# Late pairs of heads: split numerators, GpSimd low parts, queries ranked one pair earlier, one set of inputs

## The chip, the cores and the metric

The kernel runs on one core of one Trainium2 chip. Its engines are TensorE (PE in the profile, with its weight loads shown apart as PEld), VectorE (DVE), ScalarE (ACT), GpSimd (POOL) and SyncE (SP), which here only starts DMAs. The metric is the device time of one execution in microseconds; lower is better.

## The reference

First a linear attention with exponential features over 8 batches, 8 heads, 576 tokens and head size 64, then a gated feed-forward layer over the 4608 tokens that come out (width 512, hidden width 1536). All of it is float32.

```python
def phi(x):
    proj = np.einsum('bhsd,df->bhsf', x, w_phi)              # 64 -> 128 features
    proj = proj - np.max(np.abs(proj), axis=-1, keepdims=True)
    return np.concatenate([np.exp(proj), np.exp(-proj)], axis=-1)
q_p, k_p = phi(q), phi(k)
kv  = einsum('bhsf,bhsd->bhfd', k_p, v);  z = k_p summed over s
num = einsum('bhsf,bhfd->bhsd', q_p, kv)
den = einsum('bhsf,bhf->bhs', q_p, z)[..., None] + 1e-06
x   = num / den                                              # 4608 x 512
g   = x @ w_gate
out = (silu(g) * (x @ w_val)) @ w_out
```

## The kernel before

**Parts.** TensorE multiplies either float32, which it records as two instructions for each product, or `float32r`, one instruction. For a product in `float32r` that keeps the accuracy, both factors are written as a high part (a rounding copy) and a low part (value minus high part), and three products are added: high by high, low by high, high by low. The feed-forward layer has been done so throughout; the attention in parts of it.

**Attention.** Two heads make a pair, and there are 32 pairs, four for each batch. `attention(i, rank)` (from line 370) writes out pair i. The key side: load keys and values, project the keys in three groups into PSUM, find the largest magnitude (L447), subtract it (L452), two exponentials (L456, L457), products with the values into one PSUM bank `ps_kv` (L465, L472), then copy the sums out to `kvs` (L493, called `kvc`). The query side of a late pair: for each head a high part by ScalarE (L551) and a low part by VectorE (L553) into `qs`, two projections, copies to `qx` by ScalarE (L566), transpose, reduce, six tiny operations over groups of partitions (L582 to L587), transpose back (L591), subtract (L594), two exponentials (L596, L598) into `qe` and `qx`. Then the numerators and denominators: for each head two parts of 288 tokens, each of them two float32 products of `kvs` with `qe` and `qx`; ScalarE copies them out (L620, L622); VectorE divides (L629 to L633). The result is stored to DRAM or split into `xh` and `xl` (L655, L657).

**Early and late.** Pairs 0 to 7 are early and use float32 and another query path. Pairs 8 to 31 are late: keys (from pair 9) and queries are split into parts, the numerators are float32. Late pairs use two sets of inputs `kin`, `qin`, `vf` in turn, two sets of `qx`, `qe` and of `kvs`, and one set of `ks`, `qs`.

**Order.** All steps are given to a planner (`Plan`) with the engine, an assumed cost, what they wait for, and a rank. It runs through an assumed time line, and each engine always takes the ready step of lowest rank; the resulting order is what each engine then executes, strictly in that order. A late pair's steps have the pair's number as rank; steps that free a PSUM bank have a rank near -0.8 (`freeing`), feed-forward steps off TensorE -1 or -0.5. Feed-forward products on TensorE have ranks above 1000, so that they fill what the attention leaves free. Late pairs have two PSUM banks (`work`) for projections and numerators together; a step with `take` holds one until the step with `give`.

**Stages.** Early pairs come first, then the weights are decoded from float64, while feed-forward products of the first chunks of 384 tokens fill TensorE; then the late pairs with products of chunks 0 to 5; then chunks 6 to 11, two at a time, with seven products in place of eight (`pair`, L1006), for which GpSimd makes combined weights (L913, L918) and VectorE and ScalarE combined inputs (L951 to L955). These may only begin after the last step of the attention (`ended`). SBUF of the stages is shared in areas `m1`, `m2`, `a1`, `a2` by `view(tag, shape, dtype, when)`.

Of the kernel before, what the change touches and what calls it, by code (L numbers as in the profile page):

```python
# [17 lines left out]
P = 128  # L18
S = 576
# [29 lines left out]
ROOM = {"m1": 6912, "m2": 5140, "a1": 2432, "a2": 2048}  # L49
URGENT = -0.8  # L50
T_SETS = 2
# [144 lines left out]
def favor_attention_moe(ctx: ExitStack, tc: tile.TileContext, qT, kT, v, w_phi, wg, wv, wo, out):  # L196
# [58 lines left out]
    kvs = [view("m2", [4 * P]) for _ in range(2)]  # L255
    qy = [view("m2", [4, NF]) for _ in range(2)]
# [11 lines left out]
    shared = [view("a1", [2 * DM], U32) for _ in range(2)] + [view("a2", [2 * DM]) for _ in range(2)]  # L268
    raw = [t.rearrange("p (n t) -> p n t", t=2) for t in shared[:2]]
    we, wa = ([t[:, i * DM:(i + 1) * DM] for i in range(2)] for t in shared[2:])  # L270
    ks, qs = view("a1", [2, SK], F32R, 1), view("a1", [2, S], F32R, 1)
    for t, shape in ((kin, [SK]), (qin, [SK]), (vf, [5, 2, D2])):
        t[1] = view("a2", shape, F32, 1)
# [97 lines left out]
    def attention(i, rank):  # L371
# [4 lines left out]
        one = 0 if early else j  # L376
# [4 lines left out]
        if i == EARLY_PAIRS + 1:  # L381
            def clear():
                nc.gpsimd.memset(vf[1]()[:, :, :, D:], 1.0)
                for h in range(2):
                    nc.gpsimd.memset(vf[1]()[h * D:(h + 1) * D, 4, 1 - h], 0.0)
                    nc.gpsimd.memset(kin[1]()[h * D:(h + 1) * D, 4 * P + (1 - h) * D:4 * P + (2 - h) * D], 0.0)

            last["vf", i - 2] = last["kin", i - 2] = last["qin", i - 2] = add("POOL", 1000, clear, weights_done, rank)
        before = lambda name: [last.get((name, i - (1 if i <= EARLY_PAIRS else 2)))]

        k_in = [add("SP", P * 4 * P * 4, lambda: nc.sync.dma_start(get(kin[one])[:, :4 * P], kT[b, pr, :, :4 * P]),
                    before("kin"), rank)]
        k_in += [add("SP", P * P, lambda r=slice(h * D, (h + 1) * D), c=4 * P + h * D: nc.sync.dma_start(
            get(kin[one])[r, c:c + D], kT[b, pr, r, 4 * P:]), before("kin"), rank) for h in range(2)]
        if early:
            q_in = [add("SP", P * 4 * P * 4, lambda: nc.sync.dma_start(get(qin[one])[:, :4 * P], qT[b, pr, :, :4 * P]),
                        before("qin"), rank)]
            q_in += [add("SP", P * P, lambda r=slice(h * D, (h + 1) * D), c=4 * P + h * D: nc.sync.dma_start(
                get(qin[one])[r, c:c + D], qT[b, pr, r, 4 * P:]), before("qin"), rank) for h in range(2)]
        else:  # L400
            q_in = [add("SP", P * S * 4, lambda: nc.sync.dma_start(get(qin[one])[:, :S], qT[b, pr]), before("qin"), rank)]
# [10 lines left out]
        if plain:  # L412
            k_ready = k_in
        else:
            k_hi = add("ACT", act(SK), lambda: nc.scalar.copy(ks()[:, 0], get(kin[one])),
                       [*k_in, last.get(("khi", i - 1)), *weights_done], rank)
            k_lo = add("DVE", dve(SK), lambda: vec.tensor_tensor(
                out=ks()[:, 1], in0=get(kin[one]), in1=ks()[:, 0], op=ALU.subtract), [k_hi], rank)
            k_ready = [k_hi, k_lo]
            last["kin", i] = k_lo  # L420
        kv_steps = []
        for g, (t0, t1) in enumerate(GROUPS):
# [9 lines left out]
            def project(t0=t0, t1=t1, key=key, tail=tail):  # L432
                o = work[plan.bank[key]]
                for t in range(t0, t1):
                    c = slice(t * P, (t + 1) * P)
                    acc = o[:, :NF] if tail else o[:, (t - t0) * 256:(t - t0 + 1) * 256]
                    if plain:
                        matmuls([(acc, get(kin[one])[:, c], wst if tail else wbd, True, True)])
# [6 lines left out]
            kproj = add("PE", w * (pe32(width) if plain else 3 * pe(width)), project, k_ready, rank, take=key)  # L445
# [5 lines left out]
            def centre(n=n, m=m, view=view, room=room):  # L451
# [4 lines left out]
            e0 = add("ACT", act(n * NF), lambda x=room: nc.scalar.activation(x[:, :, 0], x[:, :, 1], AF.Exp), [ksub], rank)  # L456
            e1 = add("ACT", act(n * NF), lambda x=room: nc.scalar.activation(x[:, :, 1], x[:, :, 1], AF.Exp, scale=-1.0),  # L457
                     [e0], rank)
            last["km", 3 * i + g] = ksub

            def values(t0=t0, t1=t1, room=room, tail=tail):
                kv_open[0] = not tail
                if tail:
                    for k in range(2):
                        nc.tensor.matmul(ps_kv[:, 2 * k * D2:2 * (k + 1) * D2], room[:, 0, k],  # L465
                                         get(vf[one])[:, 4].rearrange("p h d -> p (h d)"), start=False, stop=k == 1)
                    return
                for t in range(t0, t1):
                    for h in range(2):
                        for k in range(2):  # L470
                            o = ps_kv[:, (2 * k + h) * D2:(2 * k + h + 1) * D2]
                            nc.tensor.matmul(o, room[:, 2 * (t - t0) + h, k], get(vf[one])[:, t, h], start=t + h + k == 0, stop=False)  # L472

            kv = add("PE", 2 * n * pe32(D2), values, [e1, *v_in, last.get(("kv", i - 1)), *kv_steps[-1:]], rank)
# [24 lines left out]
        if early:  # L499
            for g, (t0, t1) in enumerate(GROUPS):  # L500
# [9 lines left out]
                def project(t0=t0, t1=t1, key=key, tail=tail):  # L510
                    o = work[plan.bank[key]]
                    for t in range(t0, t1):
                        x = get(qin[one])[:, t * P:(t + 1) * P]
# [33 lines left out]
        else:  # L547
            copies, q_lo = [], []
            for h in range(2):
                ra, rb = rows(h)  # L550
                hi = add("ACT", act(S), lambda h=h, ra=ra: nc.scalar.copy(qs()[ra, h], get(qin[one])[ra, :S]),  # L551
                         [*q_in, last.get(("qs", h, i - 1)), *weights_done], rank)
                lo = add("DVE", dve(S), lambda h=h, ra=ra, rb=rb: vec.tensor_tensor(  # L553
                    out=qs()[rb, h], in0=get(qin[one])[ra, :S], in1=qs()[ra, h], op=ALU.subtract), [hi], rank)
# [320 lines left out]
    for t in (hh, hl):  # L875
        t += [view(tag, [CH], F32R, 2) for tag in ("a1", "m1")]
# [269 lines left out]
```

## Time and profile before

| | |
|---|---|
| Time, median of 3 runs | 1262.28 us (1261.77 to 1264.46) |
| The profiled execution's own time | 1262.5 us |
| Its span from first to last instruction | 1260.7 us |
| Mean granted TensorE clock | 0.997 |
| Busy share: PE, DVE, ACT, POOL | 98%, 75%, 55%, 20% |
| Late pairs on TensorE | from about 285 us to 797 us |
| First product of chunks 6 to 11 | 826.97 us |

A group's row gives line, engine, operation, output and input tiles by name, shape and count, then busy time, mean time of one, and idle time ahead of it with what ended it. Tiles that are views of a shared area appear under the first letter of the area's name: `m` for `m1` and `m2`, `a` for `a1` and `a2`. L312 is the helper that issues most matmuls. A row of a stretch gives start and end, its length, and for each engine the busy time and the instructions. A matmul's recorded time includes its way through the array, so the spacing of starts is what one costs TensorE.

### The profile page before, as it was taken

The page shows a single profiled execution, that of the slowest core. Times are in us where ns is not written, and L with a number is a line of the kernel's source. Part 1 is how long each engine was busy: PE and PEld are TensorE (multiplying, and loading weights), DVE is VectorE, ACT ScalarE, POOL GpSimd, SP SyncE. Part 2 cuts the span into 40 slices and gives each one's busy share as a digit, 9 for nine tenths or more (in the row PEclk, how much of TensorE's full clock was granted, in tenths as well). Part 3 has the DMA queues.
Part 4 walks back from the last instruction along what each step waited for, and adds up shares of the span by engine and source line. Part 5 has one row for each costly group of instructions (what it writes and reads, how often), then busy time and mean ns, then how long its engine had stood idle before and what let it go on. Part 6 is the DMA issues. An engine that isn't in the chain of part 4 may idle for free.

```text
span 1260.7 us, 19274 instructions
## 1 busy us (share of the span) xinstructions
PE 1241.0 (98%) x7008; PEld 1145.7 (91%) x7008; DVE 943.2 (75%) x1674; ACT 688.3 (55%) x1419; POOL 246.9 (20%) x306
## 2 busy tenths in 40 slices
PE   9999999999999999999999999989999999999998
PEld 8898899999888999999999999979998999989997
DVE  7997799997878888777877967586557756575553
ACT  6887333337677767666766765443334433353333
POOL 0000000000000000000000000285565665565550
PEclk9999999999999999999999999999999999999999
DMA  4433455546463424443444332632213322222211
GB/s 147 134 115 91 144 183 175 172 161 204 147 193 109 139 92 129 117 132 122 121 123 128 126 108 71 211 133 76 74 52 113 117 72 76 76 101 75 76 51 51
DMA packets 107312, 149.26 MB, mean 118 GB/s; under 512 B 52048, under 2 KB 61776, under 8 KB 107216
## 3 DMA queue, kind: packets, MB, share of 16 engines
q1 hardware_dynamic: 106752, 147.76, 37.3%
q8 instruction: 55, 0.90, 0.3%
q14 instruction: 41, 0.34, 0.1%
q10 hardware_dynamic: 464, 0.26, 0.1%
HBM read 119.67 MB, written 28.31 MB: 117 GB/s over the span
## 4 chain that ended last, share of the span: by engine, by line
PE 90%; DVE 4%; POOL 2%; DMA 1%; ACT 1%; issue 1%; SPq 0%; DVEq 0%; POOLq 0%
PE gv L312 23%; PE gv L1006 19%; PE o L312 19%; PE work L312 17%; PE kv L472 8%; PE kv L312 2%; PE kv L465 1%; POOL a L913 1%; POOL a L918 1%; DMA a<-in_wg_dram 1%; DVE m L951 0%; PE o L534 0%; DVE xl L955 0%; DMA m<-wlo_dram 0%; DVE km L447 0%
## 5 line engine op out<-in xcount | busy, mean ns | idle before, releaser
L312 PE MATMUL gv<-xh,w_hi 128*128 128x384 f32 x576 | 201.6, 350 | 1.4 <-DVE th L742 1.4
L312 PE MATMUL gv<-xl,w_hi 128*128 128x384 f32 x576 | 193.2, 335 | 0.0
L312 PE MATMUL gv<-xh,w_lo 128*128 128x384 f32 x576 | 193.2, 335 | 0.0
L1006 PE MATMUL gv<-xh,m 128*128 128x384 f32 x504 | 151.3, 338 | 2.6 <-ACT m L1014 2.5
L913 POOL TENSOR_TENSOR a<-w_hi,m 128x256 f32<-128x256 f32 x48 | 40.0, 865 | 571.9 <-DMA m<-wlo_dram 564.1
L918 POOL TENSOR_TENSOR a<-a 128x256 f32<-128x256 f32 x144 | 117.5, 816 | 8.5
L312 PEld LDWEIGHTS gv<-xh,w_hi 128*128 128x128 f32 x576 | 108.3, 188 | 5.1 <-DVE th L742 2.0
L312 PE MATMUL o<-w_hi,hh 128*128 128x512 f32 x270 | 112.1, 415 | 0.0
L913 POOL TENSOR_TENSOR a<-w_hi,w_lo 128x256 f32<-128x256 f32 x96 | 88.8, 954 | 118.2 <-DMA w_lo<-wlo_dram 96.1
L312 PEld LDWEIGHTS gv<-xl,w_hi 128*128 128x128 f32 x576 | 108.3, 188 | 3.2 <-DVE xl L657 0.2
L1017 DVE TENSOR_TENSOR a<-gv,a 128x384 f32<-128x384 f32 x72 | 39.9, 553 | 94.4 <-PE gv L1006 94.2
L312 PE MATMUL work<-m,m 128*128 128x288 f32 x408 | 109.4, 406 | 0.0
L312 PEld LDWEIGHTS gv<-xh,w_lo 128*128 128x128 f32 x576 | 108.1, 188 | 0.0
L312 PE MATMUL o<-w_hi,hl 128*128 128x512 f32 x270 | 107.1, 397 | 0.0
L1006 PEld LDWEIGHTS gv<-xh,m 128*128 128x128 f32 x504 | 93.7, 189 | 5.7 <-ACT m L1014 3.3
L312 PE MATMUL o<-w_lo,hh 128*128 128x512 f32 x243 | 95.7, 394 | 0.0
L312 PEld LDWEIGHTS work<-m,m 128*128 128x128 f32 x408 | 76.5, 189 | 17.1
L1006 PE MATMUL gv<-xh,w_hi 128*128 128x384 f32 x216 | 73.7, 341 | 7.5 <-DVE a L1017 4.9
L765 ACT CAST hh<-th 128x384 fp32r<-128x384 f32 x108 | 55.3, 512 | 44.0 <-DVE th L745 30.6
L472 PEld LDWEIGHTS kv<-m,m 128*128 128x128 f32 x640 | 75.8, 192 | 2.5 <-ACT m L457 0.8
L472 PE MATMUL kv<-m,m 128*128 128x66 f32 x640 | 75.6, 273 | 0.8 <-ACT m L457 0.6
L1006 PE MATMUL gv<-xl,w_hi 128*128 128x384 f32 x216 | 73.4, 340 | 0.0
(183 smaller groups left out, 2958.9 us busy)
## 6 DMA issues: line engine op xcount, KB each, us to landing
w_lo<-wlo_dram SPq DMA_DIRECT2D x60, 512.0 KB, 3.6
w_lo<-wlo_dram SPq DMA_DIRECT2D x78, 256.0 KB, 3.1
wlo_dram<-w_lo SPq DMA_DIRECT2D x36, 256.0 KB, 2.1
out_dram<-osb SPq DMA_DIRECT2D x30, 256.0 KB, 2.7
a<-in_wg_dram SPq DMA_DIRECT2D x12, 512.0 KB, 3.7
a<-in_wv_dram SPq DMA_DIRECT2D x12, 512.0 KB, 3.6
a<-in_wo_dram SPq DMA_DIRECT2D x12, 512.0 KB, 3.6
m<-wlo_dram SPq DMA_DIRECT2D x12, 512.0 KB, 3.6
```

Source lines behind the costliest of these rows:

```text
L312: nc.tensor.matmul(o, l, r, start=a, stop=z)
L465: nc.tensor.matmul(ps_kv[:, 2 * k * D2:2 * (k + 1) * D2], room[:, 0, k], get(vf[one])[:, 4].rearrange("p h d -> p (h d)"), start=False, st ...
L472: nc.tensor.matmul(o, room[:, 2 * (t - t0) + h, k], get(vf[one])[:, t, h], start=t + h + k == 0, stop=False)
L765: s4 = add("ACT", act(CH), lambda: nc.scalar.copy(get(hh[b]), th[j]), [made, hid_free[b]], FIRST)
L913: gp.tensor_tensor(out=full()[:, block(n)], in0=hi[:, block(n)], in1=get(low)[:, block(n)], op=ALU.add)
L918: gp.tensor_tensor(out=x[:, block(o)], in0=x[:, block(l)], in1=x[:, block(r)], op=ALU.subtract)
L1006: nc.tensor.matmul(o[:, :CH], l, r, start=begin and i == 0, stop=i == len(terms) - 1, skip_group_check=True)
L1017: return add("DVE", dve(CH), lambda: vec.tensor_tensor(out=snap[n](), in0=bank_c[:, :CH], in1=snap[n](), op=ALU.add), after, FIRST)
```

## The change

It concerns late pairs, apart from where views lie.

- **Numerators.** `kvs` becomes a high part `kvh` (ScalarE, from PSUM) and a low part `kvl` (VectorE, PSUM minus `kvh`), one set instead of two, made at `freeing` rank. For each head, `qe` and `qx` are copied to high parts `qh` (ScalarE) and their low parts `ql` are made by GpSimd; there is one set of these for both heads. Each part of 288 tokens then takes six `float32r` products instead of two float32 ones. `qx` is free after the low parts instead of after the numerators.
- **GpSimd.** The low parts of keys and queries move from VectorE to GpSimd.
- **Query copies** out of PSUM move from ScalarE to VectorE.
- **Ranks.** Steps of a late pair get one of five offsets; that of the query projections (`rq`) is -1, the others 0.
- **Waits.** A key projection takes its bank only once the feature buffer that it will fill is free, and a query projection only once `qx` is.
- **One set of inputs.** `kin`, `qin`, `vf` are no longer doubled for late pairs; each load waits for the pair before. The GpSimd memsets for the second set go.
- **Areas.** `a2` goes, `b1` comes; the views of the last stage are spread otherwise.

```diff
-ROOM = {"m1": 6912, "m2": 5140, "a1": 2432, "a2": 2048}
+ROOM = {"m1": 6912, "m2": 3096, "a1": 4096, "b1": 2048}
+OFFSETS = (0, -1, 0, 0, 0)
...
+    qh, ql = ([view("a1", [S], F32R, 1) for _ in range(2)] for _ in range(2))
+    kvh, kvl = view("a1", [4 * P], F32R, 1), view("b1", [4 * P], F32R, 1)
...
+        rk, rq, rm, rn, rt = (rank + (0 if early else o) for o in OFFSETS)
...
-        before = lambda name: [last.get((name, i - (1 if i <= EARLY_PAIRS else 2)))]
+        before = lambda name: [last.get((name, i - 1))]
...
-            k_lo = add("DVE", dve(SK), lambda: vec.tensor_tensor(
-                out=ks()[:, 1], in0=get(kin[one]), in1=ks()[:, 0], op=ALU.subtract), [k_hi], rank)
+            k_lo = add("POOL", pool2(SK), lambda: nc.gpsimd.tensor_tensor(
+                out=ks()[:, 1], in0=kin[0], in1=ks()[:, 0], op=ALU.subtract), [k_hi], rk)
...
-            kproj = add("PE", w * (pe32(width) if plain else 3 * pe(width)), project, k_ready, rank, take=key)
+            kproj = add("PE", w * (pe32(width) if plain else 3 * pe(width)), project,
+                        [*k_ready, *([] if early else [last.get(("kp", 3 * i + g - 2))])], rk, take=key)
...
             kvc.append(add("ACT", act(4 * D), lambda ones=ones: nc.scalar.copy(
-                cut(kvs[j], ones), sums(ones)), [kv_steps[-1], *use("kvs")], rank))
+                cut(kvs[j] if early else kvh(), ones), sums(ones)),
+                [kv_steps[-1], *(use("kvs") if early else [last.get(("kvs", i - 1)), *weights_done])], freeing))
+        if not early:
+            for ones in range(2):
+                kvc.append(add("DVE", dve(4 * D), lambda ones=ones: vec.tensor_tensor(
+                    out=cut(kvl(), ones), in0=sums(ones), in1=cut(kvh(), ones), op=ALU.subtract),
+                    [kvc[ones], last.get(("kvs", i - 1))], freeing))
...
-                lo = add("DVE", dve(S), lambda h=h, ra=ra, rb=rb: vec.tensor_tensor(
-                    out=qs()[rb, h], in0=get(qin[one])[ra, :S], in1=qs()[ra, h], op=ALU.subtract), [hi], rank)
+                lo = add("POOL", pool2(S), lambda h=h, ra=ra, rb=rb: nc.gpsimd.tensor_tensor(
+                    out=qs()[rb, h], in0=qin[0][ra, :S], in1=qs()[ra, h], op=ALU.subtract), [hi], rq)
...
-                    pj = add("PE", 2 * pe(SH), project, [lo], rank, take=key)
-                    copies.append(add("ACT", act(SH), lambda h=h, c=c, key=key: nc.scalar.copy(
+                    pj = add("PE", 2 * pe(SH), project, [lo, *use("qx")], rq, take=key)
+                    copies.append(add("DVE", dve(SH), lambda h=h, c=c, key=key: vec.tensor_copy(
                         qx[j][:, h, c], work[plan.bank[key]][:, :SH]), [pj, *use("qx")], freeing, give=key))
...
+                            terms += [(kvh()[:, n], qh[k]()[:, c]), (kvl()[:, n], qh[k]()[:, c]), (kvh()[:, n], ql[k]()[:, c])]
...
-                nu = add("PE", 2 * pe32(SH), numerators, [*done[h], *kvc, nu], rank, take=key)
+                if not early and part == 0:
+                    for k in range(2):
+                        g0 = add("ACT", act(S), lambda k=k, h=h: nc.scalar.copy(qh[k](), (qe, qx)[k][j][:, h]),
+                                 [(f0, f1)[k][h], nu or last.get(("nu", i - 1)), *weights_done], rn)
+                        done[h] += [g0, add("POOL", pool2(S), lambda k=k, h=h: nc.gpsimd.tensor_tensor(
+                            out=ql[k](), in0=(qe, qx)[k][j][:, h], in1=qh[k](), op=ALU.subtract), [g0], rn)]
+                nu = add("PE", 2 * pe32(SH) if early else 6 * pe(SH), numerators, [*done[h], *kvc, nu], rn, take=key)
...
-        last["qx", i], last["qx'", i] = nu, None
+        last["qx", i], last["qx'", i] = (nu, None) if early else (done[0][-1], done[1][-1])
...
-    t_low, t_high = ([view("m1", [8 * P], F32R, 2) for _ in range(T_SETS)] for _ in range(2))
+    t_low, t_high = ([view("a1", [8 * P], F32R, 2) for _ in range(T_SETS)] for _ in range(2))
...
-    temps = [view("m2", [2, CH], F32, 2) for _ in range(6)]
+    temps = [view("m1", [2, CH], F32, 2) for _ in range(6)]
...
-    lo_bufs = [view("m1", [8 * P], F32R, 2) for _ in range(LOW_SETS - LO_SETS)] + [flat(t) for t in w1_lo]
+    lo_bufs = [view("b1", [8 * P], F32R, 2) for _ in range(LOW_SETS - LO_SETS)] + [flat(t) for t in w1_lo]
```

More of the change, by code (lines that the diff above doesn't have):

```diff
@@ L254, in favor_attention_moe @@
     kp = [view("m1", [2, 2, 2, NF]) for _ in range(2)]
-    kvs = [view("m2", [4 * P]) for _ in range(2)]
-    qy = [view("m2", [4, NF]) for _ in range(2)]
+    kvs = [view("b1", [4 * P]) for _ in range(2)]
+    qy = [view("b1", [4, NF]) for _ in range(2)]
     kin, qin = [view("m2", [SK])] * 2, [view("m2", [SK])] * 2
@@ L265, in favor_attention_moe @@
     osb = sb("osb", [P, DM], F32, 2)
[L268 removed]
+    shared = [view("a1", [2 * DM], U32) for _ in range(2)] + [view("a1", [2 * DM]) for _ in range(2)]
     raw = [t.rearrange("p (n t) -> p n t", t=2) for t in shared[:2]]
     we, wa = ([t[:, i * DM:(i + 1) * DM] for i in range(2)] for t in shared[2:])
[L271 to L273 removed]
+    ks, qs = view("a1", [2, SK], F32R, 1), view("b1", [2, S], F32R, 1)
+    qh, ql = ([view("a1", [S], F32R, 1) for _ in range(2)] for _ in range(2))
+    kvh, kvl = view("a1", [4 * P], F32R, 1), view("b1", [4 * P], F32R, 1)
     def bank(name):
@@ L414, in attention @@
         else:
-            k_hi = add("ACT", act(SK), lambda: nc.scalar.copy(ks()[:, 0], get(kin[one])),
-                       [*k_in, last.get(("khi", i - 1)), *weights_done], rank)
-            k_lo = add("DVE", dve(SK), lambda: vec.tensor_tensor(
-                out=ks()[:, 1], in0=get(kin[one]), in1=ks()[:, 0], op=ALU.subtract), [k_hi], rank)
+            k_hi = add("ACT", act(SK), lambda: nc.scalar.copy(ks()[:, 0], kin[0]),
+                       [*k_in, last.get(("khi", i - 1)), *weights_done], rk)
+            k_lo = add("POOL", pool2(SK), lambda: nc.gpsimd.tensor_tensor(
+                out=ks()[:, 1], in0=kin[0], in1=ks()[:, 0], op=ALU.subtract), [k_hi], rk)
             k_ready = [k_hi, k_lo]
@@ L437, in project @@
                     if plain:
-                        matmuls([(acc, get(kin[one])[:, c], wst if tail else wbd, True, True)])
+                        matmuls([(acc, kin[0][:, c], wst if tail else wbd, True, True)])
                     else:
@@ L471, in values @@
                             o = ps_kv[:, (2 * k + h) * D2:(2 * k + h + 1) * D2]
-                            nc.tensor.matmul(o, room[:, 2 * (t - t0) + h, k], get(vf[one])[:, t, h], start=t + h + k == 0, stop=False)
-            kv = add("PE", 2 * n * pe32(D2), values, [e1, *v_in, last.get(("kv", i - 1)), *kv_steps[-1:]], rank)
+                            nc.tensor.matmul(o, room[:, 2 * (t - t0) + h, k], vf[0][:, t, h], start=t + h + k == 0, stop=False)
+            kv = add("PE", 2 * n * pe32(D2), values, [e1, *v_in, last.get(("kv", i - 1)), *kv_steps[-1:]], rk)
             last["kp", 3 * i + g] = kv
@@ L512, in project @@
                     for t in range(t0, t1):
-                        x = get(qin[one])[:, t * P:(t + 1) * P]
+                        x = qin[0][:, t * P:(t + 1) * P]
                         matmuls([(o[:, :NF], x, wst, True, True) if tail else
@@ L550, in attention @@
                 ra, rb = rows(h)
-                hi = add("ACT", act(S), lambda h=h, ra=ra: nc.scalar.copy(qs()[ra, h], get(qin[one])[ra, :S]),
-                         [*q_in, last.get(("qs", h, i - 1)), *weights_done], rank)
-                lo = add("DVE", dve(S), lambda h=h, ra=ra, rb=rb: vec.tensor_tensor(
-                    out=qs()[rb, h], in0=get(qin[one])[ra, :S], in1=qs()[ra, h], op=ALU.subtract), [hi], rank)
+                hi = add("ACT", act(S), lambda h=h, ra=ra: nc.scalar.copy(qs()[ra, h], qin[0][ra, :S]),
+                         [*q_in, last.get(("qs", h, i - 1)), *weights_done], rq)
+                lo = add("POOL", pool2(S), lambda h=h, ra=ra, rb=rb: nc.gpsimd.tensor_tensor(
+                    out=qs()[rb, h], in0=qin[0][ra, :S], in1=qs()[ra, h], op=ALU.subtract), [hi], rq)
                 q_lo.append(lo)
@@ L571, in attention @@
             turns = [add("DVE", dve(S), lambda h=h: vec.transpose(qe[j][:, h], qx[j][:, h]),
-                         [*copies[2 * h:2 * h + 2], *use("qe")], rank) for h in range(2)]
+                         [*copies[2 * h:2 * h + 2], *use("qe")], rm) for h in range(2)]
             per_head = lambda f: [(lambda h=h: f(h)) for h in range(2)]
```

74 lines of the change are left out of this document (34 added, 40 removed).

## The prediction

> **What bounds the kernel now.** I read the page's chain of waits first, shares of the span by engine, then busy time by stretch (PE, PEld, DVE, ACT, POOL).
>
> ```profile
> PE 90%; DVE 4%; POOL 2%; DMA 1%; ACT 1%; issue 1%; SPq 0%; DVEq 0%; POOLq 0%
> ```
>
> ```profile
> 285.00:797.00 512.00, 512.00 (x3074) 468.89 (x3073) 405.88 (x776) 349.60 (x757) 0.00 (x0) 1.00 0.42 128
> 797.00:827.00 30.00, 27.47 (x144) 25.14 (x142) 20.62 (x26) 10.14 (x17) 14.38 (x13) 0.99 0.63 216
> ```
>
> TensorE sets the end: the chain is 90% PE. In the stretch of the late pairs, the first row, PE is busy for all of 512 us, at the full granted clock (1.00). That is 512 / 24 = 21.3 us a pair, in which VectorE works 405.88 / 24 = 16.9 us (79%), ScalarE 14.6 us, GpSimd nothing. The waits in that stretch say the same from the other side:
>
> ```profile
> PEld work L312 <- DVE m L452: 0.4, 2, 0.2
> ```
>
> ```profile
> DVE m L629 <- ACT m L622: 35.6, 14, 4.7
> ```
>
> TensorE's weight loads waited 0.4 us in all, while VectorE waited 35.6 us for the copies of the numerators alone. The attention is ready when TensorE reaches it, so work taken from TensorE here shortens the run, as long as that stays so.
>
> **The products: what they cost and will cost.** The time line of PE around two heads' numerators, and query projections already made of parts:
>
> ```profile
> 603.72 2.10 PE L312 MATMUL work<-m,m 128*128 128x288 f32 x8
> 605.44 0.61 PE L312 MATMUL o<-w_hi,hh 128*128 128x512 f32 x1
> 605.89 0.39 PE L312 MATMUL o<-w_lo,hh 128*128 128x512 f32 x1
> 606.12 0.40 PE L312 MATMUL o<-w_hi,hl 128*128 128x512 f32 x1
> 606.35 2.10 PE L312 MATMUL work<-m,m 128*128 128x288 f32 x8
> 608.08 0.55 PE L312 MATMUL gv<-xh,w_hi 128*128 128x384 f32 x1
> 608.47 0.34 PE L312 MATMUL gv<-xl,w_hi 128*128 128x384 f32 x1
> 608.64 0.34 PE L312 MATMUL gv<-xh,w_lo 128*128 128x384 f32 x1
> 608.82 0.30 PE L312 MATMUL work<-a,wst_hi 128*128 128x288 f32 x1
> ...
> 609.09 0.34 PE L312 MATMUL gv<-xh,w_hi 128*128 128x384 f32 x1
> ...
> 609.61 0.29 PE L312 MATMUL work<-a,wst_hi 128*128 128x288 f32 x1
> ...
> 609.87 0.34 PE L312 MATMUL gv<-xh,w_hi 128*128 128x384 f32 x1
> ```
>
> A head's numerators now take 605.44 - 603.72 = 1.72 us and 608.08 - 606.35 = 1.73 us. The product right behind them is late too: it holds TensorE for 0.45 us (605.44 to 605.89) where its neighbour takes 0.23, and 0.39 us (608.08 to 608.47) where the next takes 0.17. So a head costs 1.725 + 0.22 = 1.945 us, and 48 heads 93.4 us. After, a head takes 12 products of 288 columns. Those of the query projections, each with a new stationary operand as here, take two in 0.27 us (608.82 to 609.09) and two in 0.26 (609.61 to 609.87), 0.1325 us each; 48 x 12 x 0.1325 = 76.3 us. No switch between kinds is left behind them. **TensorE saves 93.4 - 76.3 = 17.1 us**, 0.7 us a pair. The count of the other products is the same.
>
> **VectorE and ScalarE.** Rows from the groups by form:
>
> ```profile
> L452 DVE TENSOR_TENSOR m<-work,km 128x512 f32<-128x512 f32 x55 | 38.0, 691 | 2.2
> L566 ACT COPY m<-work 128x288 f32<-128x288 f32 x96 | 36.5, 402 | 17.9 <-PE work L312 16.9
> L596 ACT ACTIVATE m<-m 128x576 f32<-128x576 f32 x48 | 31.7, 682 | 11.3 <-DVE m L594 11.2
> L553 DVE TENSOR_TENSOR a<-a,a 64x576 fp32r<-64x576 f32 x24 | 18.1, 753 | 0.7
> L553 DVE TENSOR_TENSOR a<-m,a 64x576 fp32r<-64x576 f32 x24 | 18.1, 753 | 2.5 <-ACT a L551 1.7
> L417 DVE TENSOR_TENSOR a<-a,a 128x640 fp32r<-128x640 f32 x12 | 9.8, 818 | 0.4 <-ACT a L415 0.4
> L417 DVE TENSOR_TENSOR a<-m,a 128x640 fp32r<-128x640 f32 x11 | 9.0, 819 | 0.1
> L452 DVE TENSOR_TENSOR m<-work,km 128x128 f32<-128x128 f32 x31 | 8.6, 276 | 0.2
> ```
>
> VectorE loses the low parts, 18.1 + 18.1 + 9.8 + 9.0 = 55.0 us. It gains 96 query copies of 288 columns out of PSUM; between the two L452 rows a column costs (691 - 276) / 384 = 1.08 ns, so a copy is 276 + 160 x 1.08 = 449 ns and all are 43.1 us; and 48 subtractions of 256 columns at 276 + 128 x 1.08 = 414 ns, 19.9 us. Sum: +8 us, 0.3 us a pair. ScalarE loses the 36.5 us of L566 and gains 96 high parts of 576 at 682 ns, 65.5 us: +29 us, or 1.2 us a pair on 14.6. Neither is on the path while TensorE finds its operands ready; uncovered, they would add 1.5 us a pair, 36 us.
>
> **GpSimd.** It has no work in this stretch now; its only large operation is in the last stage:
>
> ```profile
> L918 POOL TENSOR_TENSOR a<-a x144: 727/739/1457, 811.4 to 1226.2; 128x256 f32<-128x256 f32 x144
> ```
>
> Undisturbed it takes 727 ns for 256 columns. For 576 that gives 1.64 us if all of it grows with the columns, and 0.65 us more than 727 ns, 1.38 us, if it grows at twice VectorE's 1.08 ns; I take 1.55, near the upper end, and 1.7 for 640. Each late pair puts six of the first and one of the second on GpSimd: 11 us a pair, 262 us in all, in a 21 us period. It keeps up. But a head's numerators now follow two copies and two low parts in series (0.68 + 2 x 1.55 = 3.8 us), twice per pair, since the second head reuses `qh` and `ql`: 7.6 us more of latency. The other pair in flight covers it (16.9 us of VectorE work per pair); uncovered it costs 182 us.
>
> **What GpSimd takes from VectorE.** VectorE's lines in the last stage (least, median and longest ns):
>
> ```profile
> L1025 DVE SCALAR_TENSOR_TENSOR th<-th,m x36: 550/1086/1097, 833.5 to 1243.9; 128x384 f32<-128x384 f32 x36
> L1025 DVE SCALAR_TENSOR_TENSOR th<-th,gv x36: 539/554/555, 838.7 to 1249.5; 128x384 f32<-128x384 f32 x36
> L955 DVE TENSOR_TENSOR xl<-m,xh x18: 948/1484/1497, 811.8 to 1117.2; 128x768 fp32r<-128x768 f32 x18
> ```
>
> With both inputs in SBUF and GpSimd at work, 384 columns take 1086 ns in place of 550, and 768 columns 1484 in place of 948. The loss is 536 ns for either length, so it is a wait for one GpSimd instruction, not a lower rate. With one input in PSUM (`gv`) there is none. The Trainium skill, "SBUF — State Buffer", section "Who interferes with whom", has this as a rule: a VectorE instruction with two SBUF inputs and a GpSimd one that reads SBUF take one shared port in turn, each for its whole length. These rows agree (536 of GpSimd's 727 ns).
>
> In the late stretch the exposed instructions of a pair are the two of L594, L633, some 2.3 of L766 and two tiny ones of L582 to L587. If half of the seven GpSimd instructions of a pair meet one and hold it for half of 1.55 us, that is 7 x 0.5 x 0.78 = 2.7 us a pair; bounds 0 and 7 x 1.55 = 11 us. VectorE then has 16.9 + 0.3 + 2.7 = 19.9 us of work in a period of 20.6 (21.3 - 0.7). Its present idle time, 512 - 406 = 106 us, just covers the 73 us that come. Since each engine keeps a fixed order that was planned without this wait, I count 5 us of it as reaching TensorE (bounds 0 and 65).
>
> **The rest.** With one input set a load starts when the pair before has been read. It takes 3.0 us to land and has the rest of 21 us; uncovered, 72 us. Behind it on SP stand the weight low parts, which also have their two buffers.
>
> ```profile
> m<-in_kT_dram SPq DMA_DIRECT2D x20, 256.0 KB, 3.0
> ```
>
> The new waits ahead of projections hold no more than a bank now does, and ScalarE's sums (L493) now also wait for the numerators of the pair before, with a period to spare: nothing. The removed memsets were idle GpSimd time: nothing.
>
> **The end of the attention.** How soon can chunks 6 to 11 begin?
>
> ```profile
> 794.62 2.10 PE L312 MATMUL work<-m,m 128*128 128x288 f32 x8
> ...
> 824.05 0.40 PE L312 MATMUL o<-w_hi,hl 128*128 128x512 f32 x1
> 826.97 0.69 PE L1006 MATMUL gv<-xh,w_hi 128*128 128x384 f32 x1 [2.53 <-DVE th L742]
> ```
>
> ```profile
> 800.83 0.32 SPq L647 DMA_DIRECT2D x_dram<-m  x1
> ...
> 803.91 0.42 SPq L908 DMA_DIRECT2D m<-wlo_dram  x1
> ```
>
> ```profile
> 811.82 2.91 DVE L955 TENSOR_TENSOR xl<-m,xh 128x768 fp32r<-128x768 f32 x2
> ...
> 828.24 2.43 DVE L955 TENSOR_TENSOR xl<-m,xh 128x768 fp32r<-128x768 f32 x2
> ```
>
> The last numerators end at 797; the older products last to 824.3, a lead of 27 us, in which the result is stored, weights and inputs loaded and split. The first operands are there at 814.7, a need of 17.7 us; the fourth, which the first round also needs, at 830.7. So the need lies between 17.7 and 27 us. With the saving the products run out at 807. If the attention still ended at 797, the lead would be 10 us, and 7.5 to 17 of the 17.1 us would be lost. With d for what a late pair takes longer than 21.3 us: time = 1262.5 - 17.1 + max(0, 24 d + 7.5 to 17). The whole gain needs d of -0.3 to -0.7. The areas moved (`temps` out of the area of the stored result) may spare up to the 3.1 us from 800.83 to 803.91; I take none.
>
> **Sum.** The profiled execution took 1262.5 us (span 1260.7), 0.2 above the median of 1262.28. 1262.5 - 17.1 + 5 = 1250.4, on the median 1250.2.
>
> **Rivals.** (1) *The attention keeps its pace* (d = 0), being held by latency and VectorE rather than TensorE. For it: the 7.6 us of added latency and the added work. Against: the 35.6 us in which VectorE waited for numerators. Time 1253 to 1262, say 1258.
>
> (2) *GpSimd's turn at the port makes VectorE the bound*: slower. The wait above at 7 x 1.55 / 2 = 5.4 us a pair brings VectorE to 22.6 us, over the period; d = 1.3 by that alone, of which perhaps half in practice, since not all GpSimd work meets an exposed instruction: d = 0.6 gives 1245.4 + 14.4 + 12 = 1272. It decides from d of about 0.2, where 24 x 0.2 + 12 eats the 17. For it: GpSimd is busy half the time with instructions twice as long as those that blocked for 536 ns.
>
> (3) *The change doesn't speed the products*: 576 products, if each were held by its weight load, recorded at about 188 ns, would be 108 us, 15 more than now: 1277. Against it: the 0.1325 us spacing with a new load each time.
>
> ```profile
> L312 PEld LDWEIGHTS work<-a,wst_hi 128*128 128x128 f32 x96 | 18.1, 189 | 1.0
> ```
>
> **How the numbers follow.** Forecast 0.48, all faster; its own range is 1243 (all saved, 2 to 3 us from the areas) to 1258. Rival 1 0.20, of which half faster and half the same; rival 2 0.28 and rival 3 0.04, slower. A difference under 0.2% (2.5 us) can't be told from none. Faster 0.58, same 0.10, slower 0.32. The range takes rival 1 whole and rival 2 to a little past its middle: 1243 to 1274.
>
> **What would show it.** Right: numerators as 12 instructions 0.13 us apart, PE still full through the late stretch, and chunks 6 to 11 beginning near 810 to 815. Wrong: PE waits on POOL or DVE in that stretch (rival 2, with L594 and L633 well over 750 ns), a gap or filler products between the last old product and L1006 (rival 1), or starts 0.19 us apart (rival 3). TensorE waits of over 17 us in all would make the forecast wrong.

## The result, and the profile after

The changed kernel takes 1315.28 us (median of 4 executions, 1308.62 to 1319.72); the kernel before took 1263.18 us (4 executions, 1261.77 to 1264.46). The ratio is 1.0408, with a 95% interval of 1.0383 to 1.0433: **slower by 52 us**. The prediction was 1250.2 us, with a range up to 1274. The profiled execution took 1312.99 us, span 1311.1 us, with a mean granted clock of 0.983 against 0.997.

The chain of waits of the changed kernel, shares of the span by engine:

```profile
PE 51%; DVE 18%; ACT 2%; issue 2%; POOL 1%; DMA 1%; SPq 0%; DVEq 0%; ACTq 0%; POOLq 0%
```

It was 90% PE and 4% DVE. VectorE now stands in the chain that sets the end. Busy time by stretch, from 285 us to the first product of chunks 6 to 11, first for the kernel before and then for the changed one (after the length: PE, PEld, DVE, ACT, POOL, then granted clock):

```profile
285.00:827.00 542.00, 539.47 (x3216) 494.02 (x3214) 426.50 (x802) 359.74 (x773) 14.38 (x13) 1.00 0.43 132
```

```profile
285.00:876.00 591.00, 551.00 (x3411) 514.42 (x3411) 498.57 (x879) 385.86 (x779) 261.68 (x179) 0.97 0.41 123
```

The stretch grew by 49 us of the span's 50.4, so the loss is here. TensorE stood for 591.00 - 551.00 = 40 us where it had stood for 2.5, and it ran slower: at a mean clock of 0.97 it lost some 3% of 591, 18 us, to pieces at half rate. VectorE was busy for 498.57 of the 591 us (84%), so it was not full, though TensorE waited for it. These are TensorE's waits in the stretch, by who ended them (total, count, longest):

```profile
PE kv L466 <- ACT m L450: 13.5, 6, 3.6
PE work L313 <- DVE m L446: 10.0, 9, 2.3
PE o L313 <- DVE hl L775: 5.8, 3, 3.0
PE kv L459 <- ACT m L450: 4.4, 2, 3.3
PE work L313 <- DVE m L566: 2.9, 2, 2.6
```

No DMA and no low part of GpSimd is among them. L446 is VectorE's subtraction on the keys and L450 the exponential behind it. The next rows are VectorE's groups by form, first of the kernel before, then of the changed one (L633 became L642, L766 became L775); last comes busy time, mean ns of one, and idle time:

```profile
L594 DVE TENSOR_TENSOR m<-m 128x576 f32<-128x576 f32 x48 | 33.7, 735 | 0.0
L766 DVE TENSOR_TENSOR hl<-th,hh 128x384 fp32r<-128x384 f32 x60 | 32.8, 546 | 3.2 <-ACT hh L765 2.9
L633 DVE TENSOR_TENSOR m<-m 128x576 f32<-128x576 f32 x24 | 18.1, 754 | 0.5
L583 DVE TENSOR_TENSOR qm<-qm,qu 64x36 f32<-64x36 f32 x24 | 4.5, 188 | 0.8
L587 DVE COPY qu<-qu 64x36 f32<-64x36 f32 x24 | 4.2, 176 | 0.8
...
L584 DVE COPY qu<-qm 32x36 f32<-32x36 f32 x24 | 4.1, 171 | 0.8
```

```profile
L775 DVE TENSOR_TENSOR hl<-th,hh 128x384 fp32r<-128x384 f32 x61 | 46.5, 764 | 5.4 <-ACT hh L774 5.4
L566 DVE COPY m<-work 128x288 f32<-128x288 f32 x96 | 41.1, 447 | 10.5 <-PE work L313 7.7 <-ACT m L631 2.4
L594 DVE TENSOR_TENSOR m<-m 128x576 f32<-128x576 f32 x48 | 40.6, 879 | 0.0
L642 DVE TENSOR_TENSOR m<-m 128x576 f32<-128x576 f32 x24 | 24.5, 1020 | 0.3
...
L584 DVE COPY qu<-qm 32x36 f32<-32x36 f32 x24 | 17.0, 709 | 0.8
L582 DVE COPY qu<-qm 64x36 f32<-64x36 f32 x24 | 14.9, 620 | 0.8
L583 DVE TENSOR_TENSOR qm<-qm,qu 64x36 f32<-64x36 f32 x24 | 13.7, 571 | 0.8
```

The work is unchanged, but its instructions take longer. The large ones grew by 0.14 to 0.27 us each. The six tiny ones of L582 to L587, on 36 columns, grew most: together from 25.6 to 74.6 us. One line's own instructions (least, median and longest ns) show how:

```profile
L583 DVE TENSOR_TENSOR qm<-qm,qu x24: 186/188/1360, 298.9 to 806.3; 64x36 f32<-64x36 f32 x24
L584 DVE COPY qu<-qm x24: 170/172/1468, 299.1 to 806.5; 32x36 f32<-32x36 f32 x24
```

Half of them take what they always took, and others up to 1.47 us, which is about one GpSimd instruction:

```profile
L625 POOL TENSOR_TENSOR a<-m,a 128x576 fp32r<-128x576 f32 x96 | 140.8, 1485 | 265.9 <-ACT a L623 226.0 <-PE work L313 21.8 <-DVE hl L775 14.3
L553 POOL TENSOR_TENSOR b<-m,b 64x576 fp32r<-64x576 f32 x48 | 72.8, 1518 | 294.8 <-ACT b L551 291.1 <-PE work L313 0.4
```

One place in the time line shows the way from GpSimd to TensorE (start, duration, what; in brackets the idle time before and what ended it):

```profile
641.76 2.83 POOL L625 TENSOR_TENSOR a<-m,a 128x576 fp32r<-128x576 f32 x2
...
641.96 1.30 DVE L583 TENSOR_TENSOR qm<-qm,qu 64x36 f32<-64x36 f32 x1
643.29 1.33 DVE L584 COPY qu<-qm 32x36 f32<-32x36 f32 x1
...
645.29 0.69 DVE L441 TENSOR_REDUCE km<-work 128x4 f32<-128x512 f32 x1
646.01 0.69 DVE L446 TENSOR_TENSOR m<-work,km 128x512 f32<-128x512 f32 x1
...
646.74 0.63 ACT L450 ACTIVATE m<-m 128x512 f32<-128x512 f32 x1 [4.65 <-DVE m L446]
...
647.42 0.44 PE L466 MATMUL kv<-m,m 128*128 128x66 f32 x2 [1.92 <-ACT m L450]
```

Two GpSimd low parts run from 641.76 to 644.59. VectorE's two tiny instructions beside them end at 643.26 and 644.62, and take 1.30 + 1.33 us in place of the 0.19 + 0.17 of before: 2.27 us lost. Behind them in VectorE's fixed order stand the maximum and the subtraction for the keys, then come ScalarE's exponential and TensorE's product, which waited 1.92 us. TensorE could do nothing else meanwhile: its own order is fixed too.

### The profile page after: what moved, and what is told of

It is laid out like the page before. It is cut to its first block, busy times and chain, and to the rows that moved or that the text cites. A ratio compares the mean times of both kernels' runs of the same rounds, so it can differ in the third digit from the quotient of the medians.

```text
span 1311.1 us, 20169 instructions
## 1 busy us (share of the span) xinstructions
PE 1252.5 (96%) x7207; PEld 1165.9 (89%) x7207; DVE 1011.9 (77%) x1747; ACT 710.3 (54%) x1419; POOL 494.0 (38%) x468
## 4 chain that ended last, share of the span: by engine, by line
PE 51%; DVE 18%; ACT 2%; issue 2%; POOL 1%; DMA 1%; SPq 0%; DVEq 0%; ACTq 0%; POOLq 0%
PE gv L1015 18%; PE work L313 10%; PE o L313 10%; PE gv L313 6%; PE kv L466 4%; PE kv L313 2%; DVE hl L775 2%; DVE m L571 1%; DVE qm L579 1%; DVE m L446 1%; DVE km L441 1%; DVE qu L584 1%; DVE qu L582 1%; DVE m L642 1%; DVE qm L583 1%
## 5 line engine op out<-in xcount | busy, mean ns | idle before, releaser
L625 POOL TENSOR_TENSOR a<-m,a 128x576 fp32r<-128x576 f32 x96 | 140.8, 1485 | 265.9 <-ACT a L623 226.0
L313 PE MATMUL gv<-xh,w_hi 128*128 128x384 f32 x576 | 195.5, 339 | 0.9 <-DVE th L751 0.9
L313 PE MATMUL gv<-xl,w_hi 128*128 128x384 f32 x576 | 193.5, 336 | 0.0
L553 POOL TENSOR_TENSOR b<-m,b 64x576 fp32r<-64x576 f32 x48 | 72.8, 1518 | 294.8 <-ACT b L551 291.1
L1026 DVE TENSOR_TENSOR m<-gv,m 128x384 f32<-128x384 f32 x108 | 59.9, 555 | 124.8 <-PE gv L1015 123.7
L466 PEld LDWEIGHTS kv<-m,m 128*128 128x128 f32 x1024 | 126.7, 199 | 21.7 <-ACT m L450 17.1
L922 POOL TENSOR_TENSOR m<-w_hi,w_lo 128x256 f32<-128x256 f32 x96 | 86.6, 931 | 138.7 <-DMA w_lo<-wlo_dram 116.4
L1015 PE MATMUL gv<-xh,a 128*128 128x384 f32 x432 | 129.6, 341 | 4.3 <-ACT m L1023 4.3
L927 POOL TENSOR_TENSOR m<-m 128x256 f32<-128x256 f32 x144 | 115.5, 802 | 8.5
L313 PE MATMUL work<-a 128*128 128x288 f32 x384 | 95.8, 320 | 9.9 <-DVE m L446 9.7
L1015 PEld LDWEIGHTS gv<-xh,a 128*128 128x128 f32 x432 | 80.6, 189 | 7.3 <-ACT m L1023 5.8
L450 ACT ACTIVATE m<-m 128x512 f32<-128x512 f32 (+1 forms) x96 | 50.1, 522 | 65.7 <-DVE m L446 65.0
```

Source lines behind the costliest of these rows:

```text
L313: nc.tensor.matmul(o, l, r, start=a, stop=z)
L466: nc.tensor.matmul(o, room[:, 2 * (t - t0) + h, k], vf[0][:, t, h], start=t + h + k == 0, stop=False)
L553: lo = add("POOL", pool2(S), lambda h=h, ra=ra, rb=rb: nc.gpsimd.tensor_tensor(out=qs()[rb, h], in0=qin[0][ra, :S], in1=qs()[ra, h], op=AL ...
L625: done[h] += [g0, add("POOL", pool2(S), lambda k=k, h=h: nc.gpsimd.tensor_tensor(out=ql[k](), in0=(qe, qx)[k][j][:, h], in1=qh[k](), op=AL ...
L922: gp.tensor_tensor(out=full()[:, block(n)], in0=hi[:, block(n)], in1=get(low)[:, block(n)], op=ALU.add)
L927: gp.tensor_tensor(out=x[:, block(o)], in0=x[:, block(l)], in1=x[:, block(r)], op=ALU.subtract)
```

## The experiments

The theory to test: the loss comes from GpSimd's reads of SBUF, which hold VectorE's instructions, and of these above all the tiny ones, because each can wait for a whole GpSimd instruction. The rivals: the change made the steps' order or latency worse; VectorE simply has more work; or the planner, which did not know the real durations, wrote a bad order. All ratios are against the kernel before, run on the same chip.

A change of what the planner is told also changes the order that it writes. In experiments 1, 4 and 8 the traces list the work of TensorE, ScalarE and VectorE in the same order as in the kernel that was edited, and 5 has the order of 2. In all others the order is a new one, so their times mix the edit with it.

**1. The tiny operations as reductions.** The six operations (four copies and two maxima) become `tensor_reduce` over one input each, with the same result; two small tiles take the values side by side.

```diff
-                vec.tensor_copy(qu[0:64], qm[64:128])
-                vec.tensor_tensor(out=qm[0:64], in0=qm[0:64], in1=qu[0:64], op=ALU.max)
-                vec.tensor_copy(qu[0:32], qm[32:64])
...
+                top = lambda o, x: vec.tensor_reduce(out=o, in_=x, axis=AX.X, op=ALU.max)
...
+                top(qm[0:64, :, 1], qm[64:128, :, 0:1])
+                top(qv[0:64, :, 0], qm[0:64])
+                top(qv[0:32, :, 1], qv[32:64, :, 0:1])
...
```

> The changed kernel, with the six tiny operations over groups of partitions (three of them copies from SBUF to SBUF, ... two maxima of two SBUF inputs) written as six reductions of one SBUF input each; same values, same order, same planned cost. Theory P (VectorE waits for GpSimd's turn at the SBUF read port, and that makes TensorE wait): the six fall from about 3.1 us a pair to about 1.2, some 45 us of VectorE time in all come back, and the run gets 20 to 45 us shorter, 1270 to 1295. Rival L (the longer series of steps to each numerator makes TensorE wait, and the port waits lie in idle time): the six get faster all the same, but the run stays within 8 us of 1315.

Measured: 1261.86 us, ratio 0.9972 (0.9958 to 0.9986). VectorE's groups:

```profile
L596 DVE TENSOR_TENSOR m<-m 128x576 f32<-128x576 f32 x48 | 42.8, 922 | 0.0
...
L582 DVE TENSOR_REDUCE qv<-qm 64x36 f32<-64x72 f32 x24 | 5.3, 220 | 0.8
```

The tiny ones take 179 to 220 ns whatever GpSimd does, 27.9 us in all in place of 74.6; the large subtraction (here L596) still waits, 922 ns. With the order unchanged, some 47 us less of VectorE's time made the run 53 us shorter: the holds of the tiny six were enough to turn the change into a loss.

**2. GpSimd's instructions in four pieces.** Every low part on GpSimd becomes four instructions over a quarter of the columns; the tiny operations stay as in the changed kernel.

```diff
+PIECES = 4
+    def pieces(o, a, b, n):
+        for m in range(PIECES):
+            c = slice(m * n // PIECES, (m + 1) * n // PIECES)
+            nc.gpsimd.tensor_tensor(out=o[:, c], in0=a[:, c], in1=b[:, c], op=ALU.subtract)
...
```

> The changed kernel, with each low part that GpSimd makes cut into four instructions of a quarter of the columns (144 or 160). Theory P: a wait lasts for one GpSimd instruction, so the longest of L583 and L584 falls from 1.36 and 1.47 us to about 0.5, the mean of the tiny operations to about half of its excess, and the run gets 10 to 35 us shorter although GpSimd needs some 0.5 us more for each low part. Rival L: the series of steps gets about 1 us longer per head, so the run gets 10 us or more longer.

Measured: 1258.41 us, ratio 0.9951 (0.9933 to 0.9970). Two of the tiny lines one by one, and GpSimd's group:

```profile
L589 DVE TENSOR_TENSOR qm<-qm,qu x24: 186/422/535, 301.4 to 764.9; 64x36 f32<-64x36 f32 x24
L590 DVE COPY qu<-qm x24: 170/398/502, 301.6 to 765.3; 32x36 f32<-32x36 f32 x24
```

```profile
L376 POOL TENSOR_TENSOR a<-m,a 128x144 fp32r<-128x144 f32 x384 | 194.6, 543 | 137.4 <-ACT a L629 91.2 <-issue 12.4 <-PE work L314 10.4
```

The longest hold falls from 1360 and 1468 ns to 535 and 502, about one piece (543 ns), though more of them are held at all (the medians rise to 422 and 398). The hold is as long as GpSimd's instruction. How much of the 57 us gained comes from the shorter holds is not shown: the planner now counts 1.79 us for a low part in place of 1.55, and the order is another.

**3. The low parts on VectorE.** The three low parts that GpSimd makes go to VectorE, all else as changed.

```diff
...
-                        done[h] += [g0, add("POOL", pool2(S), lambda k=k, h=h: nc.gpsimd.tensor_tensor(
+                        done[h] += [g0, add("DVE", dve(S), lambda k=k, h=h: vec.tensor_tensor(
```

> The changed kernel, with all low parts of keys, queries and features made by VectorE (GpSimd idle in the stretch of the late pairs, as before the change). Theory P: no exposed instruction waits any more (L594 back to 735 ns, the tiny operations to 180), but VectorE has 55 + 70 us more work in the stretch, about 530 us, so it sets the pace there: 1285 to 1335. Rival L: the series is shorter (0.75 in place of 1.5 us for each low part), so the run gets 15 us or more shorter than 1315.

Measured: 1343.27 us, ratio 1.0619 (1.0599 to 1.0638). A stretch of it:

```profile
285.00:830.00 545.00, 523.28 (x3258) 492.38 (x3256) 498.79 (x963) 356.98 (x718) 0.00 (x0) 0.97 0.43 127
```

With no GpSimd work nothing is held (L594 takes 744 ns, the tiny six 25.7 us in all), but VectorE is 498.79 / 545 = 92% busy and the attention ends later still, at 882 us against 831.6. Leaving GpSimd out is no remedy: the work belongs there, in another shape.

**4. The kernel before, with GpSimd reads added.** To the kernel before, 167 GpSimd subtractions of 576 columns are added at the places where the change has its low parts; what they write is read by nothing.

```diff
+    def extra(after, rank):
+        add("POOL", pool2(S), lambda: nc.gpsimd.tensor_tensor(out=scratch, in0=some, in1=some, op=ALU.subtract), after, rank)
...
+            for f in (*f0, *f1):
+                extra([f], rank)
```

> The kernel before, with GpSimd instructions added whose result nobody reads: in each late pair six or seven subtractions of 576 columns read from SBUF, started behind the high parts and exponentials; nothing waits for them and the order of the other engines is the same. Theory P: this alone makes the tiny operations and L594, L633, L766 slower, as in the changed kernel, VectorE's busy time in the late stretch grows by 50 to 80 us, TensorE begins to wait, and the run takes 1275 to 1315. Rival L: exposed instructions slow down but it fits in VectorE's idle time, and the run stays within 5 us of 1263.

Measured: 1320.62 us, ratio 1.0445 (1.0417 to 1.0472). Groups and TensorE's longest wait:

```profile
L777 DVE TENSOR_TENSOR hl<-th,hh 128x384 fp32r<-128x384 f32 x59 | 47.9, 811 | 3.1 <-ACT hh L776 2.9
L602 DVE TENSOR_TENSOR m<-m 128x576 f32<-128x576 f32 x48 | 45.5, 979 | 0.0
...
L560 DVE TENSOR_TENSOR a<-a,a 64x576 fp32r<-64x576 f32 x24 | 25.6, 1067 | 0.7
```

```profile
PE o L318 <- DVE hl L777: 12.3, 5, 5.0
```

Nothing of the change is in this kernel but GpSimd's work, its order is that of the kernel before, and it loses about as much as the changed kernel does. Order and products of the change are therefore not needed for the loss. L560 is a low part (L553 before, 753 ns): those that stay on VectorE here are held too.

**5. Both remedies.** The reductions of 1 and the four pieces of 2 together, on the changed kernel.

> The changed kernel with both edits at once: the six tiny operations as reductions of one input, and each low part on GpSimd cut into four instructions. Theory P (port waits alone turned the change into a loss): with the tiny operations out of it, and waits of a quarter at L594, L633 (t3) and L766, TensorE's idle time in the late stretch falls under the 7.5 and 9.0 us that each edit left alone, and of the 15 us of products saved some 10 show: 1248 to 1257. If the two edits cured the same waits and something else holds the rest: 1257 to 1262, no better than the cut alone.

Measured: **1246.27 us, ratio 0.9853 (0.9839 to 0.9868)**, the fastest of all, 19 us faster than before and 69 faster than the change as it was made. The stretch, TensorE's longest wait in it, and a head's numerators:

```profile
285.00:814.50 529.50, 527.85 (x3432) 501.76 (x3431) 447.78 (x883) 387.40 (x781) 368.89 (x680) 1.00 0.47 138
```

```profile
PE o L314 <- DVE hl L783: 0.9, 1, 0.9
```

```profile
776.83 0.30 PE L314 MATMUL work<-a 128*128 128x288 f32 x1
...
778.42 0.33 PE L314 MATMUL gv<-xh,w_hi 128*128 128x384 f32 x1
778.59 0.33 PE L314 MATMUL gv<-xl,w_hi 128*128 128x384 f32 x1
```

TensorE is full again, at the full clock. GpSimd is busier than in the changed kernel (368.89 against 261.68 us), so it is not the amount of its work that hurt.

**6. Two pieces in place of four.** As 5, with `PIECES = 2`.

> As the run with both edits, but each low part in two instructions instead of four: waits of half of 1.3 us, and 0.3 us less GpSimd time for each low part. Theory P: within 3 us of the run with four, 1249 to 1258; if GpSimd's longer time for four pieces had become a cost of its own, this one is faster by over 3 us.

Measured: 1256.66 us, ratio 0.9927 (0.9904 to 0.9951): between one piece (experiment 1) and four, each in an order of its own.

**7. The query rank.** As 5, with `OFFSETS` all 0, so that queries are no longer ranked with the next older pair.

> The run with both edits, and all rank offsets 0, so that queries are ranked with their own pair again. If the offset is what made the attention end earlier among the products (a lead of 44 us in the changed kernel, 27 before), the lead falls back towards 27 us and the time rises by up to 10 us; if the port waits were the whole difference, the time stays within 3 us.

Measured: 1274.53 us, ratio 1.0081 (1.0064 to 1.0098), 28 us slower than 5; more than I expected.

```profile
PE gv L1023 <- ACT xh L971: 13.8, 2, 9.0
```

TensorE is hardly held while the attention lasts (3.0 us of 524 without work), but the last numerators come at 808.9 us (778.3 in 5) and the old products run out at 815.8. So chunks 6 to 11 find no operands: the lead is 6.9 us in place of 36.

**8. The kernel before, with GpSimd writes added.** At each of the places of 4 stand two memsets of 577 ns each: 193 us of GpSimd that only writes. One execution, 1268.38 us, beside a median of 1265.19 of the kernel before; so there is no interval.

```diff
-        add("POOL", pool2(S), lambda: nc.gpsimd.tensor_tensor(out=scratch, in0=some, in1=some, op=ALU.subtract), after, rank)
+        add("POOL", pool2(S), lambda: [nc.gpsimd.memset(scratch, 0.0) for _ in range(2)], after, rank)
```

> The kernel before with GpSimd instructions whose result nobody reads, in the same places as in the run with added reads, but they only write (two fills of 576 columns each in place of one subtraction). If what VectorE waits for is the read side of the port: L594, L633 and L766 keep their 735, 753 and 540 ns, and the run stays within 5 us of the kernel before. If any GpSimd work blocks VectorE: they grow as in the run with added reads, in proportion to GpSimd's busy time, and the run takes 1270 or more. The tiny copies from SBUF to SBUF may still wait if they use the write side too.

```profile
L602 DVE TENSOR_TENSOR m<-m 128x576 f32<-128x576 f32 x48 | 33.7, 735 | 0.0
L595 DVE COPY qu<-qu 64x36 f32<-64x36 f32 x24 | 8.5, 354 | 0.8
L591 DVE TENSOR_TENSOR qm<-qm,qu 64x36 f32<-64x36 f32 x24 | 4.5, 188 | 0.8
```

Instructions with two inputs in SBUF are untouched (735 and 188 ns, as before). The tiny copies still wait: L595, the last of the six, takes 354 ns in place of L587's 176. So GpSimd's writes alone can hold VectorE's copies, and the two-input instructions are held only by one that reads.

**9. Eight pieces.** As 5, with `PIECES = 8`.

> As the run with both edits (1246), but each low part in eight pieces of 72 or 80 columns. Theory P: an exposed instruction waits for half as long as with four, but it meets as many; GpSimd's fixed time of some 0.3 us a piece makes a low part 1 us longer or more and keeps the port as busy. So little is left to gain: 1243 to 1256. Over 1260 would say that GpSimd's own time now sets the pace.

Measured: 1286.88 us, ratio 1.0187 (1.0152 to 1.0222).

```profile
PE work L314 <- POOL a L376: 13.9, 12, 2.2
```

```profile
L376 POOL TENSOR_TENSOR a<-m,a 128x72 fp32r<-128x72 f32 x768 | 261.7, 379 | 79.4 <-ACT a L631 54.5 <-PE work L314 14.1 <-issue 4.1
```

A piece of 72 columns takes 379 ns, one of 144 took about 550: eight pieces make 3.0 us where one instruction took 1.5. Now TensorE waits for the low parts themselves.

**10. The planner told the real durations.** The changed kernel, with the planner's costs set to what its trace shows.

```diff
-            mg = add("DVE", 6 * 170, over_groups, [*mx, last.get(("back", i - 1))], rm)
+            mg = add("DVE", 3110, over_groups, [*mx, last.get(("back", i - 1))], rm)
...
-            qc = [add("DVE", dve(S), f, [back[h]], rm) for h, f in enumerate(per_head(lambda h: vec.tensor_tensor(
+            qc = [add("DVE", 879, f, [back[h]], rm) for h, f in enumerate(per_head(lambda h: vec.tensor_tensor(
...
```

> The changed kernel as it was (long GpSimd instructions, tiny copies), with only the planner's costs changed: the six tiny operations at the 3110 ns that they took in the changed kernel's trace, L594 at 879, L633 (t3) at 1020, L766 at 766. Theory P has two forms. If the waits hurt because the fixed order was planned without them (TensorE stands at a step whose operands come late while products wait behind it), planning with them puts more products ahead and wins back most of the loss: 1262 to 1285. If VectorE simply has no time left for them, the attention ends later, the old products run out and the loss stays: 1295 to 1320.

Measured: 1318.89 us, ratio 1.0429 (1.0412 to 1.0447), no better than the changed kernel. TensorE is now at work for 515.4 of the 526 us up to 811, but then:

```profile
811.00:867.00 56.00, 32.08 (x146) 27.34 (x145) 28.49 (x48) 25.79 (x54) 18.40 (x15) 0.65 0.18 59
```

The order now uses up the old products earlier, by about 815 us, and TensorE stands at the end of the attention instead of in its middle. The tiny six still take 68.6 us. The assumed costs are not the cause; VectorE's lost time is.

The table sets side by side what VectorE lost to waits and what the run lost. The loss is worked out per kernel as count times (mean less the mean before) over the tiny six, L594, L633, L766 and L657 (the low part of the result) and their successors; in experiment 4 also over the low parts of L417 and L553, which VectorE still makes there. For the changed kernel it is 49.0 + 6.9 + 6.4 + 13.3 + 3.0.

| Kernel | Tiny six, us | L594, ns | VectorE's loss, us | Ratio to before |
|---|---|---|---|---|
| changed | 74.6 | 879 | 79 | 1.0408 |
| 1, reductions | 27.9 | 922 | 36 | 0.9972 |
| 2, four pieces | 48.6 | 900 | 44 | 0.9951 |
| 5, both | 27.9 | 924 | 25 | 0.9853 |
| 6, two pieces | 27.9 | 858 | 30 | 0.9927 |
| 4, reads in the kernel before | 43.8 | 979 | 79 | 1.0445 |

Three pairs of kernels have one order and can be compared directly. From 5 to 2, 18 us more of loss (43.7 against 25.4) cost 12 us of time; from 1 to the changed kernel, 43 us cost 53; from the kernel before to 4, 79 us cost 56.

Of the ranges on record only those of 8 and 10 held. Runs 1, 2 and 5 came out faster than theory P's range, and 3 and 4 slower than it; 6 lay 10 us from the run with four pieces in place of 3, 7 rose by 28 us in place of up to 10, and 9 passed the 1260 that it named as the sign of GpSimd's own time setting the pace.

## Why the prediction was wrong

**The products: right.** 0.1325 us each and 1.59 us a head were predicted. The changed kernel's last head and the end of its attention, time line of PE:

```profile
830.01 0.30 PE L313 MATMUL work<-a 128*128 128x288 f32 x1
...
831.61 0.39 PE L313 MATMUL o<-w_hi,hh 128*128 128x512 f32 x1
...
876.02 0.40 PE L313 MATMUL o<-w_hi,hl 128*128 128x512 f32 x1
876.25 0.34 PE L1015 MATMUL gv<-xh,w_hi 128*128 128x384 f32 x1
```

A head takes 831.61 - 830.01 = 1.60 us, in experiment 5 1.59, and the product behind it there takes its usual 0.17 us: no switch is left. **Rival 3 is refuted**, and nearly all of the saving of 17.1 us is there: in experiment 5, with 1.65 us of gaps in the stretch, the span is 16.4 us shorter than before (1244.3 against 1260.7), 12.5 of it in the stretch.

**Durations: right.** The query copy took 447 ns (449 predicted); GpSimd 1485 and 1518 ns for 576 columns (1.55). (The lower of the two estimates behind that 1.55 had a slip: 320 columns at twice 1.08 ns are 0.69 us and not 0.65, so 1.42 and not 1.38; nothing hangs on it.) Single input sets show no cost: no DMA is among TensorE's waits.

**The port: right in kind, wrong in place, and near in size partly by luck.** The sum took 2.7 us a pair, between 0 and 11; it is 79 / 24 = 3.3. But it was made of "the two of L594, L633, some 2.3 of L766 and two tiny ones of L582 to L587". These lost about 1.8 us a pair (26.6 us and a third of 49, by 24). All six tiny ones wait, the copies too, and they make 49 of the 79 us: being short doesn't shorten a wait for a whole GpSimd instruction. The Trainium skill, "SBUF — State Buffer", section "Who interferes with whom", which the prediction used for two inputs only, also says that copies can use the shared ports, so that they may be held too, and that `tensor_reduce` never contends. The traces agree with both: the copies at 709 ns, the reductions at 179 to 220.

**The step that failed: "I count 5 us of it as reaching TensorE (bounds 0 and 65)".** From one start to the next in PE's time line, against the median of the same product, I work out for the changed kernel's 591 us: 523.7 us of products at full rate, some 49 us of standing in 65 places, 17 us of half rate, 1.5 of rest. So 66 us were lost where the sum had 5, just over the upper bound. In experiment 1, the same order without holds on the tiny six, the same working gives about 12 and 1.4 us: most of the 66 came through these six. Two things were wrong. The idle time of 106 us that "just covers the 73 us" is a mean over a stretch; each wait falls in front of what stands next in a fixed order, here often the keys' maximum and subtraction (nine waits for L446, and eight for the exponential behind it), and idle time elsewhere does not give it back. And the clock had no term: most waits of 2 us or more cost a piece at half rate on top.

**The formula for the end: right, where TensorE is kept fed.** It gives 1245.4 + max(0, 24 d + 7.5 to 17), with 24 d the shift of the last numerators from 797. In experiment 5 these come at 778.3, 24 d is -18.7, and the formula gives 1245.4; the profiled execution took 1246.1. In experiment 7 they come at 808.9, 24 d is 11.9: 1265 to 1274, and 1271.5 was measured. So the price of the lead was well seen, but that of the rank was not: the sum had no term for the offset of -1, and without it experiment 5 takes 28 us more.

For the changed kernel the formula fails. The last numerators come at 831.6, so it gives 1287 to 1297, and 1313.0 was measured: it takes TensorE to work at full rate all the while. **Rival 1 is refuted**: the old products lasted to 876.25, 44.6 us past the last numerators, and L1015 follows with no gap. TensorE was not out of products; it was held in the midst of them, with products left that stood behind the waiting ones in its order.

**Rival 2 was what happened in kind**, with its place and its sign; its price was not. It has VectorE set the pace once its work exceeds the period of 20.6 us. That work stayed under it: from 285 us to the last numerators VectorE was busy for 474.84 us, 19.8 a pair. The attention still took (831.6 - 285) / 24 = 22.8 us a pair, since the waits struck singly and in full. The rival gave d = 0.6 and 1272 us; the last numerators came 34.6 us later, d = 1.44, and the standing and the half rate of TensorE, which it did not count, came on top.

## What to carry to other kernels

Before work goes to GpSimd, look at every VectorE instruction that can run beside it: an operation with two inputs in SBUF, or a copy in SBUF, can be held for one whole GpSimd instruction, however small it is itself, and a chain of tiny ones can be held again and again. Write tiny ones as reductions, cut GpSimd's instructions so that a hold is short but their fixed cost small (here four pieces of 543 ns did best, with an order planned for them; eight were too many), and check that what is behind them in a fixed order can wait. Idle time summed over a stretch covers a stall only if the order has other ready work at that very place.

## What the runs showed of the hardware

The clock fell after waits of only 2 us. In the changed kernel's time line and stretches:

```profile
622.35 0.69 PE L466 MATMUL kv<-m,m 128*128 128x66 f32 x2 [2.03 <-ACT m L450]
```

```profile
622.30:629.10 6.80, 6.75 (x29) 6.59 (x30) 4.25 (x7) 3.67 (x7) 0.00 (x0) 0.50 0.01 2
```

TensorE waited 2.03 us, and from about the end of that wait the granted clock was 0.50 for 6.8 us; the wait of 1.92 us at 647.42, shown above, was followed by 3.4 us of the same from 649.6. The stretch has twelve waits of 1.87 to 3.58 us, each with no other wait of over 0.3 us in the 6.8 us before it. Eight of them were followed by such a piece, four (1.87, 1.99, 2.16 and 2.36 us) were not, and no shorter wait was. So a single wait of 2 us can suffice, but need not; what decides between the two these runs do not show. The Trainium skill, "TensorE: Matmul & The Clock Gate", section "HAM oscillation — how this bites in real kernels", gives gaps over about 3.4 us as what to avoid; here gaps of 2 us were enough, so the trace does not agree with that figure as a safe limit.

A GpSimd subtraction has a large fixed part in these kernels: it takes 379 ns for 72 columns, 543 for 144 and 1485 for 576. The first two differ by 2.3 ns a column, which leaves about 0.2 us that does not depend on the columns, an estimate.
